# Two token tiles of three half batches by seven block products of half width, in a fused attention and feed-forward kernel

## The chip, the cores and the metric

The kernel runs on one core of one Trainium2 chip. A core has five engines, each with its own instruction queue: TensorE (PE in the profile, with its weight loads as PEld), VectorE (DVE), ScalarE (ACT), GpSimd (POOL) and SyncE (SP), whose queue issues most of the DMA transfers. The metric is the time of one execution in microseconds (us), as the median over runs. Matmul results lie in PSUM banks, which the kernel holds as tiles of 128 x 512 fp32.

## The reference

Two stages, one after the other. Attention is masked by clusters: each query and key goes to the nearest of 16 centroids of its head, and a query sees only keys of its own cluster. The feed-forward stage applies two weight matrices with SiLU between them.

```python
batch, n_heads, seq, head_dim = (4, 8, 768, 64)
...
q_assign = np.argmax(np.einsum('bhsd,hcd->bhsc', q_n, c_n), axis=-1)
k_assign = np.argmax(np.einsum('bhsd,hcd->bhsc', k_n, c_n), axis=-1)
mask = q_assign[:, :, :, None] == k_assign[:, :, None, :]
scores = np.where(mask, scale * np.matmul(q, k.transpose(0, 1, 3, 2)), -1e9)
attn = softmax(scores) @ v
x = np.ascontiguousarray(attn.transpose(0, 2, 1, 3)).reshape(B * S, H * D)   # 3072 x 512
h = x @ w_in                                                                 # 512 x 2048
out = (h * (1.0 / (1.0 + np.exp(-h)))) @ w_out                               # 2048 x 512
```

## The kernel before

**Tiling.** The work is cut into eight half batches (b, c): batch b of 4, half c of its 768 tokens, 384 tokens each. For each half batch and head pair there are score units (`qk_mm`, two matmuls `pS` of 384 columns), an exponential each on ScalarE (`exp`, tile `P`), the product with the values (`pv`, tile `pO`, 36 matmuls of 65 columns), a normalisation on VectorE (`norm`) and a transpose into `xts` (`xn_d` by DMA, or `xn_t` and `xn_ev`). There are 192 score units, 24 per half batch, numbered in order.

The feed-forward stage of a half batch has two kinds of pieces. A hidden unit `unit_a` is one of 16 blocks of 128 hidden features: four matmuls `ph` of 384 columns, tanh on ScalarE, and a gate on VectorE that writes the block into `gt` (f16, 16 blocks x 384 tokens). A part `part_b` is a quarter of an output tile of 128 tokens x 512 columns: four matmuls `po` with a block of `gt` as weights and 512 columns of `wout_s` streaming. Four parts make one tile, VectorE copies it from PSUM with a factor 0.5 into `ot`, and SP stores it. A half batch has three such tiles (`NM` = 3).

**Cluster codes.** For each query and key job a load (`load`, tile `raw`), a split into two f16 halves (`hi`, `lo`, tile `hl`), a transpose by DMA (`xpose`, tile `ab`), logits (`psN`), sums, maxima and comparisons on VectorE, and a way back into `ab` (`cd_mm` and `cd_ev`, or for later jobs `c_scale` on GpSimd, `c_xpose` on SP, `c_move` on GpSimd) give the mask, which is added by the same matmul that makes the scores.

**Order.** Up to the first 26 or so score units the order is a list written out by hand (`plan`). From there a planner in Python emits the instructions: it keeps a clock per engine, lists of pieces with a ready time, a length and a due time (`add`, `run`), and for TensorE chooses at each step among scores, transposes, hidden units and parts (`options`). Loads and the jobs' chains are dated by the number of a score unit (`date`). The spacing of score units is steered by `PACE`. What the planner emits is fixed in the program; on the chip each engine works off its own queue in that order and waits on semaphores.

**Buffers.** Four PSUM banks (`free`) go round among `ph`, `po`, `pO`, `psN`, `psC` and `px`; two double banks hold the scores. `raw` has eight buffers, `hl` four, `ot` three, `gt` two.

**End.** After the last scores the remaining parts are put between the hidden units of half batch (3,1) (`unit_aa` makes two blocks at once), then its three output tiles follow, the last one in three column pieces (L986).

## Time and profile before

| what | us |
|---|---|
| median of 3 runs | 305.29 |
| lowest and highest run | 304.9, 306.08 |
| span of the profiled execution | 302.8 |
| TensorE busy in it | 294.3 |
| ScalarE busy | 211.2 |
| VectorE busy | 200.6 |
| GpSimd busy | 69.1 |

The span runs from the first to the last instruction of the program in one profiled execution; the run times hold in addition what lies before and after it. A row of the timeline gives a start, a length, engine, source line, operation, tiles and count. The length of a matmul is that of one pass through the array, and matmuls overlap: how fast they follow each other is read from their starts. A row of the list of groups gives the count, then busy time and the mean length of one in ns, then the engine's idle time before such instructions and what ended it.

### The profile page before, as it was taken

The numbers are of one execution on the slowest core, as the hardware profiler recorded it, in microseconds if no ns is written. First come the engines' busy times: TensorE is split into PE (matmuls) and PEld (weight loads), VectorE is DVE, ScalarE is ACT, GpSimd is POOL, SyncE is SP. The second block draws the span as 40 slices with busy tenths as digits, with TensorE's granted clock in tenths as the row PEclk, the third lists the DMA queues.
The fourth block names the chain that finished last, engine by engine and source line by source line (L and its number), as shares of the span: only waits on it lengthen the run. The fifth ranks groups of instructions, "written<-read, shape, count | busy, mean of one in ns | idle before, by whom it ended". The sixth has DMA issues, their size and how long they took to land.

```text
span 302.8 us, 7783 instructions
## 1 busy us (share of the span) xinstructions
PE 294.3 (97%) x3113; PEld 186.3 (62%) x3113; DVE 200.6 (66%) x427; ACT 211.2 (70%) x341; POOL 69.1 (23%) x131
## 2 busy tenths in 40 slices
PE   7899989999999999999999999999999999999995
PEld 3777756566675566655666556655666556755644
DVE  5987669699995679855889468873464136522732
ACT  5899889653985688955698468955897568951520
POOL 2984700101310141433333324122100000000000
PEclk9999999999999999999999999999999999999999
DMA  7888999999794879869999998953101120010102
GB/s 212 249 185 183 201 254 209 247 252 223 174 184 117 218 188 151 197 160 176 231 187 226 187 179 211 163 82 97 38 0 55 46 82 13 16 50 35 37 35 69
DMA packets 74387, 44.07 MB, mean 146 GB/s; under 512 B 54352, under 2 KB 69360, under 8 KB 74352
## 3 DMA queue, kind: packets, MB, share of 16 engines
q1 hardware_dynamic: 69264, 35.16, 50.8%
q0 software_dynamic: 4800, 8.13, 14.2%
q8 instruction: 24, 0.39, 0.6%
q10 hardware_dynamic: 288, 0.30, 0.3%
q14 instruction: 11, 0.09, 0.1%
HBM read 27.30 MB, written 6.29 MB: 111 GB/s over the span
## 4 chain that ended last, share of the span: by engine, by line
PE 87%; ACT 4%; DVE 4%; DMA 2%; SPq 1%; issue 1%; DVEq 0%; ACTq 0%
PE ph L410 25%; PE po L468 25%; PE pS L343 19%; PE pO L360 11%; PE psN L175 3%; ACT P L348 3%; PE phs L448 2%; DVE hl L127 1%; PE po L986 1%; DMA raw<-in_k_dram 1%; DMA xt<-xn 1%; SPq L107 1%; ACT ab L159 1%; PE px L382 0%; SPq L228 0%
## 5 line engine op out<-in xcount | busy, mean ns | idle before, releaser
L348 ACT ACTIVATE P<-pS 128x768 f16<-128x768 f32 x192 | 155.6, 821 | 55.1 <-PE pS L343 54.7
L343 PE MATMUL pS<-ab 128*128 128x384 f16 x384 | 93.2, 326 | 0.5 <-ACT P L348 0.4
L410 PE MATMUL ph<-xt,win_s 128*128 128x384 f16 x480 | 92.4, 326 | 1.2 <-DVE gt L433 0.8
L468 PE MATMUL po<-wout_s,gt 128*128 128x512 f16 x368 | 90.8, 379 | 0.0
L433 DVE SCALAR_TENSOR_TENSOR gt<-tn,ph 128x384 f16<-128x384 f32 x120 | 64.0, 549 | 23.7 <-ACT tn L430 23.1
L430 ACT ACTIVATE tn<-ph 128x384 f32<-128x384 f32 x120 | 60.1, 507 | 10.1 <-PE ph L410 8.1
L410 PEld LDWEIGHTS <-win_s 128*128 128x128 f16 x480 | 46.2, 98 | 31.4 <-issue 2.0
L468 PEld LDWEIGHTS <-gt 128*128 128x128 f16 x368 | 35.0, 98 | 33.8
L343 PEld LDWEIGHTS <-ab 128*128 128x128 f16 x384 | 34.7, 98 | 26.1 <-issue 1.1
L360 PEld LDWEIGHTS <-P 128*128 128x128 f16 x1152 | 39.8, 97 | 4.4
L360 PE MATMUL pO<-vt,P 128*128 128x65 f16 x1152 | 41.2, 193 | 0.0
L127 DVE SCALAR_TENSOR_TENSOR hl<-raw,hl 128x768 f16<-128x768 f32 (+3 forms) x35 | 31.9, 916 | 0.8 <-ACT hl L118 0.4
L475 DVE TENSOR_SCALAR ot<-po 128x512 f32<-128x512 f32 x23 | 15.8, 688 | 23.3 <-PE po L468 23.1
L290 POOL CAST vt<-vn 128x384 f16<-128x384 f32 x32 | 17.9, 558 | 46.4 <-DMA vn<-in_v_dram 41.9
L187 DVE TENSOR_REDUCE L<-psN 128x192 f32<-128x384 f32 (+1 forms) x27 | 14.9, 550 | 15.1 <-PE psN L175 15.0
L232 POOL DMA_DIRECT2D ab<-cdt x16 | 8.9, 557 | 58.0 <-PE pS L343 28.0
L175 PEld LDWEIGHTS <-ab 128*128 128x128 f16 x458 | 17.2, 97 | 5.0 <-DMA ab<-hl 1.1
L175 PE MATMUL psN<-stk,ab 128*128 128x32 f16 (+1 forms) x458 | 18.6, 188 | 0.5 <-DMA ab<-hl 0.5
L370 DVE RECIPROCAL zr<-pO 128x6 f32<-128x6 f32 x32 | 6.2, 193 | 19.2 <-PE pO L360 18.8
L372 DVE TENSOR_TENSOR xn<-pO,zr 128x384 f16<-128x384 f32 x32 | 17.8, 557 | 1.1
L219 POOL TENSOR_SCALAR od<-od 128x96 f16<-128x96 f16 x16 | 9.2, 576 | 36.0 <-DVE od L212 35.9
L122 DVE TENSOR_SCALAR hl<-raw 128x768 f16<-128x768 f32 x24 | 13.9, 580 | 0.6 <-DMA raw<-in_k_dram 0.6
(75 smaller groups left out, 155.8 us busy)
## 6 DMA issues: line engine op xcount, KB each, us to landing
raw<-in_k_dram SPq DMA_DIRECT2D x31, 192.0 KB, 3.8
out_dram<-ot SPq DMA_DIRECT2D x23, 256.0 KB, 2.3
raw<-in_q_dram SPq DMA_DIRECT2D x24, 192.0 KB, 3.6
vn<-in_v_dram SPq DMA_DIRECT2D x16, 192.0 KB, 4.5
vn<-in_v_dram POOLq DMA_DIRECT2D x16, 192.0 KB, 3.7
win_s<-in_moe_w_in_dram POOLq DMA_DIRECT2D x8, 256.0 KB, 6.7
wout_s<-in_moe_w_out_dram POOLq DMA_DIRECT2D x4, 512.0 KB, 18.2
raw<-in_q_dram SPq DMA_DIRECT2D x2, 384.0 KB, 4.3
```

Of the source, the lines that this page charges most:

```text
L127: nc.vector.scalar_tensor_tensor(out=hl[:, s, 1, :], in0=raws[job.name][:, s, :], scalar=QS, in1=hl[:, s, 0, :], op0=ALU.mult, op1=ALU.sub ...
L175: nc.tensor.matmul(L[:, n % g, :, n // g], ab[:, i, :], stk[:, job.groups[i // 3][0], x : x + w], start=(x == 0), stop=(x + w == 2 * HC),)
L290: nc.gpsimd.tensor_copy(vt[:, :, 0:D], vns.pop(i))
L343: nc.tensor.matmul(pS[:, e, 0:HALF], abs_[kj.name][:, kn, :], rhs, start=True, stop=True)
L348: nc.scalar.activation(out=P, in_=pst.pop(u)[:, :, 0:HALF], func=AF.Exp, bias=0.0, scale=ESC)
L360: nc.tensor.matmul(o[:, (2 * t + h) * VW : (2 * t + h + 1) * VW], Ps[i + h, c, j // 2][:, j % 2, ts(t, 128)], vtb[(i + h) % 13][:, j, 0:VW ...
L372: nc.vector.tensor_tensor(out=xn, in0=ov[:, :, 0:D], in1=zr.unsqueeze(2).to_broadcast([128, 2 * NM, D]), op=ALU.mult)
L410: nc.tensor.matmul(ph[:, 0:HALF], win_s[:, r, ts(fb, 128)], xts[b, c][:, r, :], start=(r == 0), stop=(r == NR - 1))
L430: nc.scalar.activation(out=tn, in_=ph[:, 0:HALF], func=AF.Tanh, bias=0.0, scale=0.5)
L433: nc.vector.scalar_tensor_tensor(out=gt[:, fb, :], in0=tn, scalar=1.0, in1=ph[:, 0:HALF], op0=ALU.add, op1=ALU.mult)
L468: nc.tensor.matmul(po, gts[b, c][:, fc, ts(t, 128)], wout_s[:, fc, :], start=(fc == 0), stop=(fc == NFB - 1))
L475: nc.vector.tensor_scalar(out=ot, in0=po, scalar1=0.5, scalar2=None, op0=ALU.mult)
```

## The change

In the half batches (2,0), (2,1) and (3,0), two of the three token tiles (256 tokens) are no longer made by 2 x 4 parts, but by seven products of Strassen's scheme in Winograd's form. `gt` of the two tiles is seen as a 2 x 2 block matrix (token tile by half of the hidden features), `wout_s` as 2 x 2 (half of the hidden features by half of the 512 output columns). A product is eight matmuls of 256 columns over half of the hidden features (`Pair.product`). Six products add up in one PSUM bank X, in the order 1, 6, 5, 7, 4, 3, and product 2 goes to a second bank Y; between them ScalarE and VectorE read the banks (`p1`, `c11`, `u2`, `c22`, `c12`), as the partial sums are the outputs. The third tile of these half batches is still made by four parts, which the planner may put between the products.

What the products need beside is made on VectorE: four sums of `gt` blocks per pair (`Pair.sums`, 128 x 1024 f16 each, two of them in place), and once the four sums of `wout_s` blocks (`tw_piece`, ten instructions over 32 blocks of 128 x 256), from score unit 122 on. The weights' sums lie in the buffers `raw0` to `raw4` and in `zz`, a copy of X in `hl3`; the loads from the 19th on therefore turn in `raw5` to `raw7`, their halves in `hl0` to `hl2`, and the two code tiles share four buffers.

The factor 0.5 of the output moves into the values' column of ones, which becomes 2, so that the attention output is halved; tanh takes scale 1.0, and the output is copied unscaled. In the planner some pieces of VectorE may go to ScalarE (`either`), some constants have other values (`PACE` 1.34 in place of 1.40), and products have their own rules. The three last output tiles are made as before.

```diff
+    EARLY = H + 2 + H
+
+    def raw_tag(n):
+        return f"raw{n % 8 if n < EARLY else 5 + n % 3}"
 
     def load(job, eng=nc.sync):
-        raw = mp.tile([128, 12, D], f32, name="raw", tag="raw", bufs=8)
+        n = len(raws)
+        raw = mp.tile([128, 12, D], f32, name="raw", tag=raw_tag(n), bufs=1)
         for dst, ap in job.srcs:
...
+            n = len(hls)
+            hls[job.name] = mp.tile([128, 12, 2, D], f16, name="hl", tag=f"hl{n % 4 if n < EARLY else n % 3}", bufs=1)
...
-        def act():
+        def act(eng="D"):
             ot = mp.tile([128, DM], f32, name="ot", bufs=3)
-            nc.vector.tensor_scalar(out=ot, in0=po, scalar1=0.5, scalar2=None, op0=ALU.mult)
+            if eng == "A":
+                nc.scalar.activation(out=ot, in_=po, func=AF.Copy, bias=0.0, scale=1.0)
+            else:
+                nc.vector.tensor_copy(ot, po)
             done(po)
             nc.sync.dma_start(out[b * S : (b + 1) * S, :].rearrange("(p j) d -> p j d", j=NJ)[:, j, :], ot)
...
+    HK, HD = NFB // 2, DM // 2
+    uus, tws = [], []
+    TW = ((0, 0, 6), (0, 6, 2), (1, 0, 4), (1, 4, 4), (2, 0, 2), (2, 2, 4), (2, 6, 2), (3, 0, 2), (3, 2, 4), (3, 6, 2))
+
+    def tw(n, f, m=1):
+        x = n * HK + f
+        if x < 30:
+            assert x // 6 == (x + m - 1) // 6
+            return tws[x // 6][:, x % 6 : x % 6 + m, :]
+        return zz[:, (x - 30) * HD : (x - 30 + m) * HD].rearrange("p (m e) -> p m e", m=m)
+
+    def tw_piece(n, f, m):
+        if n * HK + f < 30 and len(tws) <= (n * HK + f) // 6:
+            tws.append(mp.tile([128, 6, HD], f16, name="tw", tag=f"raw{len(tws)}", bufs=1))
+        ks, us = slice(f, f + m), slice(HK + f, HK + f + m)
+        lo_, up = slice(0, HD), slice(HD, DM)
+        a = wout_s[:, ks if n == 0 else us, lo_ if n == 3 else up]
+        b_ = tw(0, f, m) if n == 2 else tw(2, f, m) if n == 3 else wout_s[:, ks, up if n else lo_]
+        nc.vector.tensor_tensor(out=tw(n, f, m), in0=a, in1=b_, op=ALU.subtract)
+
+    def uu_tile():
+        uus.append(mp.tile([128, DM + HD], f32, name="uu", tag="hl3", bufs=1))
+        nc.gpsimd.memset(uus[0][:, 0:HD], 0.0)
+
+    class Pair:
+
+        def __init__(self, b, c):
+            self.b, self.c, self.gt = b, c, gts[b, c]
+
+        def sums(self, k):
+            gt = self.gt
+            if k == 1:
+                self.sg = mp.tile([128, 2, HK, 128], f16, name="sg", tag="sg", bufs=1)
+            low, high = slice(0, HK), slice(HK, NFB)
+            a11, a12 = gt[:, low, 128:256], gt[:, high, 128:256]
+            a21, a22 = gt[:, low, 0:128], gt[:, high, 0:128]
+            s1, s2 = self.sg[:, 0], self.sg[:, 1]
+            o, x, y, op = (
+                (s1, a21, a22, ALU.add), (s2, s1, a11, ALU.subtract), (a21, a11, a21, ALU.subtract), (a12, a12, s2, ALU.subtract)
+            )[k - 1]
+            nc.vector.tensor_tensor(out=o, in0=x, in1=y, op=op)
+
+        def product(self, k):
+            gt, lo_, up = self.gt, slice(0, HD), slice(HD, DM)
+            if k == 1:
+                self.X = bank("po")
+            if k == 2:
+                self.Y = bank("po2")
+            o = self.Y[:, lo_] if k == 2 else self.X[:, up if k in (5, 3) else lo_]
+            for f in range(HK):
+                if k in (5, 6):
+                    w, x = self.sg[:, k - 5, f, :], tw(0 if k == 5 else 2, f)[:, 0, :]
+                else:
+                    fc = f if k in (1, 7) else HK + f
+                    w = gt[:, fc, 0:128] if k in (4, 7) else gt[:, fc, 128:256]
+                    x = tw(3 if k == 4 else 1, f)[:, 0, :] if k in (4, 7) else wout_s[:, fc, up if k == 3 else lo_]
+                nc.tensor.matmul(o, w, x, start=(f == 0 and k in (1, 2)), stop=(f == HK - 1), skip_group_check=True)
+
+        def p1(self):
+            self.ot = mp.tile([128, DM], f32, name="ot", bufs=3)
+            nc.scalar.activation(out=self.ot[:, HD:DM], in_=self.X[:, 0:HD], func=AF.Copy, bias=0.0, scale=1.0)
+
+        def c11(self):
+            nc.vector.tensor_tensor(out=self.ot[:, HD:DM], in0=self.Y[:, 0:HD], in1=self.ot[:, HD:DM], op=ALU.add)
+            done(self.Y)
+
+        def u2(self):
+            nc.scalar.activation(out=uus[0][:, HD : HD + DM], in_=self.X, func=AF.Copy, bias=0.0, scale=1.0)
+
+        def rows(self):
+            o = out[self.b * S : (self.b + 1) * S, :].rearrange("(p j) d -> p (j d)", j=NJ)
+            return o, self.c * NM * DM
+
+        def c22(self):
+            nc.vector.tensor_tensor(out=self.ot[:, 0:HD], in0=self.X[:, 0:HD], in1=uus[0][:, DM : DM + HD], op=ALU.add)
+            o, x = self.rows()
+            nc.sync.dma_start(o[:, x + HD : x + HD + DM], self.ot)
+
+        def c12(self):
+            ot = mp.tile([128, DM], f32, name="ot", bufs=3)
+            nc.vector.tensor_tensor(out=ot, in0=self.X, in1=uus[0][:, 0:DM], op=ALU.add)
+            done(self.X)
+            o, x = self.rows()
+            nc.sync.dma_start(
+                o[:, x : x + 3 * DM].rearrange("p (a e) -> p a e", a=2)[:, :, 0:HD], ot.rearrange("p (a e) -> p a e", a=2)
+            )
...
-        nc.vector.memset(vt[:, :, D : D + 1], 1.0)
+        nc.vector.memset(vt[:, :, D : D + 1], 2.0)
...
-    PACE, LEAST, GAIN = 1.40, 12, .03
+    PACE, LEAST, GAIN, WORK = 1.34, 12, .03, 20.05
     HOLD = 6
+    MARGIN = 0.3
+    EARLY_T = 122
...
+    def backlog(eng, t):
+        return max(clock[eng] - t, 0.0) + sum(p[2] for p in lanes[eng] if p[0] <= t + 1.0)
+
+    def either(ready, dve, act, f, then=None, late=0.0):
+        eng = "ACT" if backlog("ACT", ready) + act + MARGIN < backlog("DVE", ready) + dve else "DVE"
+        add(eng, ready, act if eng == "ACT" else dve, lambda: f(eng[0]), then, late)
...
+    tw_at = {}
+    date(EARLY_T - 1, lambda t: add("POOL", t, 0.3, uu_tile))
+
+    def tw_step(n, t):
+        if n < len(TW):
+            add("DVE", t, 0.06 + 0.16 * TW[n][2], lambda: tw_piece(*TW[n]), lambda t: (tw_at.__setitem__(TW[n][:2], t), tw_step(n + 1, t)), 9.0)
+
+    def tw_ready(k):
+        n = {6: 2, 5: 0, 7: 1, 4: 3}.get(k)
+        need = [tw_at.get(x[:2]) for x in TW if x[0] == n]
+        return None if None in need else max(need, default=0.0)
+
+    date(EARLY_T, lambda t: tw_step(0, t))
...
-    turn, po_on = 0, None
+    turn, pairs, at, next_pair, later = 0, {}, {}, [], []
+    paired = {(b, c) for b in range(2, B) for c in range(2)} - {(B - 1, 1)}
...
+    def sums_from(b, c, t):
+        pr = pairs[b, c]
+
+        def step(k, t):
+            add("DVE", t, 0.65, lambda: pr.sums(k), lambda t: (tell(b, c, f"s{k}", t), step(k + 1, t) if k < 3 else None), k - 1.0)
+
+        step(1, t)
 
...
+            if fb == NFB - 1 and (b, c) in paired:
+                if all("over" in at[x] for x in pairs if x != (b, c)):
+                    sums_from(b, c, t)
+                else:
+                    next_pair.append((b, c))
...
+                if (b, c) in paired:
+                    pairs[b, c], at[b, c] = Pair(b, c), {}
+                    qb.extend([(b, c, "p", k) for k in (1, 2, 6, 5, 7, 4, 3)] + [(b, c, NM - 1, n) for n in range(4)])
+                else:
+                    qb.extend((b, c, t_, n) for t_ in range(NM) for n in range(4))
...
+    def follow(it):
+        b, c, _, k = it
+        pr = pairs[b, c]
+
+        def told(name):
+            return lambda t: tell(b, c, name, t)
+
+        def then(t):
+            tell(b, c, f"p{k}", t)
+            if k == 1:
+                add("ACT", t + 0.2, 0.40, pr.p1, told("c1"))
+            elif k == 2:
+                when(b, c, ("p2", "c1"), lambda t: add("DVE", t + 0.2, 0.45, pr.c11))
+                when(b, c, ("p2", "s2"), lambda t: add("DVE", t + 0.06, 0.65, lambda: pr.sums(4), told("s4"), 1.0))
+            elif k == 5:
+                add("ACT", t + 0.2, 0.61, pr.u2, told("u2"))
+            elif k == 7:
+                add("DVE", t + 0.2, 0.45, pr.c22, lambda t: (tell(b, c, "c22", t), sent(t)))
+            elif k == 3:
+                tell(b, c, "over", t)
+                if next_pair:
+                    sums_from(*next_pair.pop(), t)
+                add("DVE", t + 0.2, 0.69, pr.c12, sent)
+
+        return then
...
+    def part_ready(it, bank_at):
+        b, c, t_, n = it
+        if t_ != "p":
+            need = [gate_at.get((b, c, fb)) for fb in range(4 * n, 4 * n + 4)] + ([bank_at] if n == 0 else [])
+        elif n in (1, 2):
+            need = [gate_at.get((b, c, fb)) for fb in range(HK * (n - 1), HK * n)] + [bank_at]
+        else:
+            names = {6: ("c1", "s2"), 5: ("s1",), 7: ("u2", "s3"), 4: ("c22",), 3: ("c22", "s4")}[n]
+            need = [at[b, c].get(x) for x in names] + [tw_ready(n)]
+        return None if None in need else max(need)
...
-        if unit < NU and unit - 2 in exp_at and 6 * pv_next > unit - 15:
+        if unit < NU and unit - 2 in exp_at and 6 * pv_next > unit - 11:
...
-        if qb and (po_on or bank_at is not None):
-            b, c, t_, n = qb[0]
-            need = [gate_at.get((b, c, fb)) for fb in range(4 * n, 4 * n + 4)]
+        if qb:
             a_soon = qa and x_at[qa[0][:2]] <= t + 0.5
-            if None not in need and (len(qb) > HOLD or not a_soon):
-                found.append((3 if turn < 4 else 2, max(need + ([] if po_on else [bank_at])), 0.863, "b"))
+            opened = qb[0][3] != (1 if qb[0][2] == "p" else 0)
+            ahead = next((k for k, q in enumerate(qb) if (q[2] == "p") != (qb[0][2] == "p")), None)
+            for k in (0, ahead):
+                if k is not None and (k or opened or len(qb) > HOLD or not a_soon):
+                    r = part_ready(qb[k], bank_at)
+                    if r is not None:
+                        found.append((3.5 if k else 3 if turn < 4 else 2, r, 0.874 if qb[k][2] == "p" else 0.863, ("b", k)))
```

68 lines of the change are left out of this document (44 added, 24 removed).

## The prediction

> **What bounds the kernel now.** The first part of the profile page comes first, then the TensorE clock row, then the chain of work that ended last.
>
> ```profile
> span 302.8 us, 7783 instructions
> ...
> PE 294.3 (97%) x3113; PEld 186.3 (62%) x3113; DVE 200.6 (66%) x427; ACT 211.2 (70%) x341; POOL 69.1 (23%) x131
> ...
> PEclk9999999999999999999999999999999999999999
> ...
> PE 87%; ACT 4%; DVE 4%; DMA 2%; SPq 1%; issue 1%; DVEq 0%; ACTq 0%
> ```
>
> TensorE (PE) is busy for 97% of the span at full clock and makes 87% of the chain. An average can hide a stage with another limit, so the table of busy time by stretch is next. Its columns are the stretch, its length, the busy time of each engine, the clock, the DMA share and GB/s.
>
> ```profile
> 0.00:57.00 57.00, 52.67 (x707) 36.73 (x708) 44.47 (x117) 47.59 (x81) 25.24 (x42) 1.00 0.96 210
> 57.00:190.00 133.00, 132.09 (x1414) 83.29 (x1413) 103.39 (x208) 95.09 (x150) 37.82 (x75) 1.00 0.91 196
> 190.00:289.00 99.00, 99.00 (x917) 60.28 (x916) 48.80 (x97) 68.01 (x111) 6.05 (x14) 1.00 0.22 53
> ```
>
> TensorE idles in the first 57 us, whose order is written out by hand and stays. From 57 to 190 us it is idle 0.9 us, while the DMA engines are 91% busy. From 190 to 289 us it never idles, VectorE (DVE) is half free and DMA nearly empty. The three pairs that change lie in that last stretch. So the time is the sum of the matmuls' spacings, and the question is what matmuls the change removes and what waits it puts between them.
>
> "Busy" overlaps pipelined matmuls, so spacings are read from starts, in the timeline of TensorE (start, length, instruction, count):
>
> ```profile
> 240.32 1.26 PE L360 MATMUL pO<-vt,P 128*128 128x65 f16 x36
> 241.41 0.49 PE L343 MATMUL pS<-ab 128*128 128x384 f16 x2
> ...
> 244.98 1.03 PE L468 MATMUL po<-wout_s,gt 128*128 128x512 f16 x4
> 245.84 0.49 PE L343 MATMUL pS<-ab 128*128 128x384 f16 x2
> ...
> 279.82 1.46 PE L410 MATMUL ph<-xt,win_s 128*128 128x384 f16 x8
> 281.12 1.46 PE L448 MATMUL phs<-xt,win_s 128*128 128x384 f16 x8
> ...
> 288.92 7.07 PE L468 MATMUL po<-wout_s,gt 128*128 128x512 f16 x32
> 295.82 3.70 PE L986 MATMUL po<-wout_s,gt 128*128 128x320 f16 x48
> ```
>
> A 512-column matmul takes (295.82 - 288.92)/32 = 0.2156 us, its weight load included; a 384-column one (281.12 - 279.82)/8 = 0.1625; a 65-column one (241.41 - 240.32)/36 = 0.0303.
>
> **The change, part by part.** *Products.* Per pair, 32 matmuls of 512 columns (two tiles, 16 blocks) become 56 of 256 columns (7 products of 8). No row has 256 columns. From 512 and 384 the slope is 0.0531/128 = 0.000415 us a column, so 0.1625 - 128 x 0.000415 = 0.109; from 65 and 384 it is the same, 0.109. Bounds: half of the 512-column spacing, 0.1078, below; the 65-column spacing plus 191 columns at 0.2156/512, 0.111, above. I take 0.1094: a product is 0.875 us, a pair 56 x 0.1094 = 6.13 in place of 32 x 0.2156 = 6.90. Saved 0.77 a pair, **2.3 us for three** (2.1 to 2.6 by the bounds).
>
> The Trainium skill, "TensorE: Matmul & The Clock Gate", section Back-to-back issue gap, speaks against this: it gives streams of load and matmul about 81 ns at 128 columns and 131 ns at 512, so a matmul of half the width costs much more than half. Interpolated (an estimate), 256 columns would be 98 ns, a pair 5.5 in place of 4.2 us, and the change a loss of 3.9. The trace disagrees: 215.6 ns at 512, 30.3 at 65.
>
> *VectorE sums* are new: four per pair over 128x1024 f16, and 32 blocks of 128x256 f16 of the weights. No row has two f16 inputs in SBUF. The nearest (the first is the view of one line, with duration min/median/max):
>
> ```profile
> L127 DVE SCALAR_TENSOR_TENSOR hl<-raw,hl x35: 350/951/1298, 4.0 to 198.0; 128x768 f16<-128x768 f32 x26, 128x576 f16<-128x576 f32 x7, 128x384 f16<-128x384 f32 x1, 128x192 f16<-128x192 f32 x1
> ```
> ```profile
> L161 DVE COPY ab<-pTk 128x768 f16<-128x768 f16 x7 | 3.8, 549 | 0.5 <-PE pTk L150 0.5
> L433 DVE SCALAR_TENSOR_TENSOR gt<-tn,ph 128x384 f16<-128x384 f32 x120 | 64.0, 549 | 23.7 <-ACT tn L430 23.1
> L430 ACT ACTIVATE tn<-ph 128x384 f32<-128x384 f32 x120 | 60.1, 507 | 10.1 <-PE ph L410 8.1
> L348 ACT ACTIVATE P<-pS 128x768 f16<-128x768 f32 x192 | 155.6, 821 | 55.1 <-PE pS L343 54.7
> L475 DVE TENSOR_SCALAR ot<-po 128x512 f32<-128x512 f32 x23 | 15.8, 688 | 23.3 <-PE po L468 23.1
> ```
>
> Scaled by columns, a sum takes 0.549 x 1024/768 = 0.73 us at the rate of the f16 copy, or 0.951 x 1024/768 = 1.27 at that of the two-input line with an f32 input. I take 0.73, since types and layout are the copy's. The Trainium skill, "VectorE: DVE Perf Modes", section Side-by-side, lets two-input 16-bit work pass two elements a cycle; 1024 columns would be some 0.7 us (an estimate). All sums together: 12 x 0.73 + 8192 x 0.549/768 = 8.8 + 5.9 = 14.7 us. VectorE is free for 50 of the 99 us after 190, and some 30 us of matmuls stand between the scores of unit 122 and the first product that reads a sum of weights, so I cost them at nothing. Without that cover (each gate behind a sum holds a PSUM bank) a sum delays TensorE by up to its own 0.73.
>
> *Evictions.* Six of 0.688 us become three sets of two reads of PSUM by ScalarE and three by VectorE. In the changed order ScalarE (ACT) also takes four further output evictions, one code tile and one transposed block. ACT is free for 31 of the last 99 us; no cost, but each can stand ahead of an exponential (0.821) that TensorE awaits.
>
> *Waits inside a pair.* Product 6 needs the second sum. In pairs (2,1) and (3,0) the order puts a product, a score pair, a part, a product and a score pair between the last hidden unit and it: 0.875 + 0.325 + 0.862 + 0.875 + 0.325 = 3.26 us. The chain is 0.16 (matmul length 0.326 less spacing) + 0.51 tanh + 0.55 gate + 2 x 0.73 = 2.68: 0.58 to spare, or 0.24 late behind an exponential. Pair (2,0) has over 6 us there. Product 7 needs ScalarE's copy of the bank, about 0.61 us (0.507 plus 128 columns at (0.821 - 0.507)/384); in (2,1) a part and two score pairs, 1.51 us, stand before it, the chain with an exponential ahead is 0.16 + 0.82 + 0.61 = 1.59. So margins are near zero: 0 to 0.8 a pair; I take **+0.2** in all.
>
> *Smaller buffers.* The last 16 loads turn in 3 buffers in place of 8, their halves in 3 in place of 4. In SP's changed order none of those loads waits for an engine, so the transposes and stores queued behind them aren't held: no cost. A load that did wait would hold SP's whole queue.
>
> *The order from 57 us on* is made anew, with its DMA issues. TensorE lost time there only at four places: at 71, 73 and 145 us at or before a hidden unit, whose bank or input was late, and at 143 us at logits whose transposed input had not landed:
>
> ```profile
> 71.38 2.41 PE L410 MATMUL ph<-xt,win_s 128*128 128x384 f16 x12
> 73.62 0.28 PE L241 MATMUL psC<-ident,om 128*96 128x128 f16 x2
> 74.02 1.30 PE L410 MATMUL ph<-xt,win_s 128*128 128x384 f16 x7
> ...
> 142.53 0.49 PE L343 MATMUL pS<-ab 128*128 128x384 f16 x2
> 143.53 0.52 PE L175 MATMUL psN<-stk,ab 128*128 128x32 f16 x12 [0.51 <-DMA ab<-hl]
> ...
> 145.08 1.77 PE L410 MATMUL ph<-xt,win_s 128*128 128x384 f16 x8
> 146.68 0.49 PE L343 MATMUL pS<-ab 128*128 128x384 f16 x2
> ```
>
> Starts less spacings: 2.24 - 1.95 = 0.29; 0.40 less two short ones (0.11) = 0.29; 1.00 - 0.325 = 0.68; 1.60 - 1.30 = 0.30; together 1.56. For the 0.68, SP's queue shows what stood ahead of the late transpose:
>
> ```profile
> 135.47 1.17 SPq L228 DMA_TRANSPOSE cdt<-od  x1
> 136.73 0.53 SPq L477 DMA_DIRECT2D out_dram<-ot  x1
> 137.35 1.86 SPq L136 DMA_TRANSPOSE ab<-hl  x1
> ```
>
> In the changed order it stands ahead of both, up to 1.88 us sooner. Against that, matmuls counted at their spacings put the scores of unit 102 3.0 us earlier than before (133.2 in place of 136.2), so data are wanted earlier too. All gone would be -1.56, twice as much +1.56; I take **-0.3**.
>
> *Sum*, against the profiled execution's own span: 302.8 - 2.3 + 0.2 - 0.3 = 300.4. The median of the runs, 305.29, lies 2.5 above that span, for start and end that the change doesn't touch: **302.9 us**.
>
> **The rivals.**
>
> *Half-rate sums* (slower). At 1.27 us a sum, the chain to product 6 with an exponential ahead is 0.16 + 0.82 + 0.51 + 0.55 + 2.54 = 4.58, 1.32 over the 3.26, in two pairs: +2.6, so 305.29 - 2.3 + 2.6 = 305.6. It decides from 1.19 us a sum on, where two waits eat the 2.3. For it: the only two-input rows run at 1.25 ns a column (0.951/768); against it: they all read f32 or PSUM.
>
> *Data come no sooner than before* (slower). If the stretch from 57 to 190 us is held by DMA, TensorE waits out the 3.0 us by which the scores of unit 102 moved up: 305.29 - 2.3 + 3.0 = 306.0; it decides from 2.3. For it: a share of 0.91 and one wait on a transpose; against it: that was 0.68 us in 133, and loads are dated by unit, so they move up too.
>
> *The gain is waited away in the pairs* (no change): 0.6 late at product 7 or 6 in each, 1.8 in all, 304.8. For it: margins of 0.58 and -0.08; against it: exponentials are ahead only part of the time, ACT being 69% busy there (68.01 of 99).
>
> *A narrow matmul costs its weight load besides* (slower). With a load's own length added to each narrow matmul,
>
> ```profile
> L468 PEld LDWEIGHTS <-gt 128*128 128x128 f16 x368 | 35.0, 98 | 33.8
> ```
>
> a pair is 56 x 0.207 = 11.6, +4.7 each, 319.4; it decides from 6.90/56 = 0.123 us a matmul. The 65-column row, load included, excludes it. The flat spacing that the Trainium skill gives (page and section above) would fall on this side too.
>
> **How the numbers follow.** Forecast, with sums and waits as costed: 0.75. Waited away 0.11; data no sooner 0.08; half-rate 0.05; flat matmuls 0.01. About 0.5%, 1.53 us, is what a measurement here can tell from no change: under 303.76 is faster, over 306.82 slower. The forecast's own spread runs from 302.9 - 0.3 - 0.2 - 1.26 = 301.1 (2.6 saved, no waits, the whole 1.56 back) to 302.9 + 0.2 + 0.2 + 1.0 = 304.3 (2.1 saved, waits doubled, 0.7 more lost from 57 us on); nearly all of it lies under 303.76, 0.72, and half of the waited-away case, where only some of its waits fall, adds 0.06: faster 0.78. Half-rate and data cases lie about 306 and spill over 306.82 with less than half; with the flat matmuls slower is 0.07. Same is the rest, 0.15. The range, 301.4 to 304.9, holds the forecast and the waited-away case.
>
> **What would show it.** Right: 168 matmuls of 256 columns, eight of them starting 0.87 us before the next group; 272 matmuls of 512 columns left on the output line in place of 368; sums near 0.73 us; no idle row of TensorE on VectorE or ScalarE between 190 us and the end; a span near 300.4. Wrong: sums over 1.19 us; gaps before products 6, 7 or 4; starts of logits or scores after a DMA between 57 and 190 us that add to more than 2 us; a matmul spacing over 0.12.

## The result and the profile after

| | before | after |
|---|---|---|
| median of the runs, us | 305.4 (4 runs) | 312.29 (4 runs) |
| lowest and highest, us | 304.9, 306.08 | 307.86, 314.94 |
| profiled execution, us | | 307.86 |
| span of the profiled execution, us | 302.8 | 306.1 |

The changed kernel is slower in these runs: the ratio of its time to that of the kernel before is 1.0129, with a 95% interval of 1.0082 to 1.0175, where 0.992 was predicted. Three of its four runs had a mean granted clock of 0.987 to 0.994 in place of 0.999, and the two slowest of them stay out of that ratio, as does each run over 1.5% above the fastest of its kernel in every ratio below, so the median stands higher than the ratio says.

The page of the changed kernel, the lines that were shown of the kernel before:

```profile
span 306.1 us, 7968 instructions
...
PE 293.0 (96%) x3185; PEld 193.4 (63%) x3185; DVE 213.1 (70%) x446; ACT 217.5 (71%) x353; POOL 70.7 (23%) x132
...
PE 71%; DMA 13%; DVE 5%; ACT 5%; issue 3%; POOL 1%; SPq 1%; DVEq 0%; POOLq 0%; ACTq 0%
```

TensorE is busy 1.3 us less (293.0 for 294.3), and the span is 3.24 us longer (306.08 for 302.84 before rounding). The chain that ended last now runs through transfers for 13% of the span, where it was 2%, and through TensorE for 71%, where it was 87%. The busy time by stretch says where:

```profile
0.00:57.00 57.00, 51.40 (x696) 36.23 (x697) 43.74 (x115) 46.72 (x79) 25.87 (x42) 1.00 0.95 203
57.00:190.00 133.00, 129.54 (x1385) 80.90 (x1383) 104.72 (x205) 95.61 (x150) 36.72 (x73) 1.00 0.93 193
190.00:289.00 99.00, 99.00 (x1013) 68.69 (x1012) 58.89 (x117) 73.02 (x121) 8.11 (x17) 1.00 0.26 61
```

In the last stretch, where the products stand, TensorE never idles, as before. From 57 to 190 us it idles 3.46 us in place of 0.91, and in the first 57 us 5.60 in place of 4.33.

"Busy" hides part of it, so I also added up, over all matmuls, the time from one start to the next beyond the spacing that its width needs (0.2158 us at 512 columns, 0.1625 at 384, 0.1092 at 256, 0.056 at 128, 0.0303 at 65). This is called lost time below.

| lost by TensorE, us | 0 to 57 | 57 to 100 | 100 to 150 | 150 to 190 | from 190 | last start to end of span |
|---|---|---|---|---|---|---|
| before | 7.74 | 0.64 | 0.99 | 0.00 | 0.05 | 3.51 |
| after | 9.43 | 1.54 | 0.01 | 3.23 | 0.11 | 4.23 |

The sum of the spacings themselves fell by 2.38 us (the last start 301.85 - 14.32 lost, against 299.33 - 9.42; the first start, at 1.18 us, is the same in both). So the 3.24 us come out: -2.38 of matmuls, +1.69 in the first 57 us, +3.15 from 57 to 190, +0.06 behind it, +0.72 at the end.

The 4.78 us that the changed kernel loses from 57 to 190 us are for the most part of three kinds. TensorE loses 0.80 and 0.36 at 84 and 86 us ahead of matmuls that wait on a gate (the last section says what held VectorE there). It loses 1.14 and 0.36 at 154 and 157 us, again on gates, on a chain that starts at a late load. And it loses 0.67 and 1.03 where it waits on a transfer itself, once for a cluster code and once for a transposed attention output:

```profile
168.12 0.50 PE L349 MATMUL pS<-ab 128*128 128x384 f16 x2 [0.51 <-DMA ab<-cdt]
182.81 0.32 PE L416 MATMUL ph<-xt,win_s 128*128 128x384 f16 x1 [0.86 <-DMA xt<-xn]
```

The largest of these waits shows how a transfer reaches TensorE by way of VectorE. The chain of waits passes here (start, length, what):

```profile
148.36 4.24 DMA raw<-in_k_dram
152.72 0.56 DVE hl L128
153.28 0.46 DVE gt L439
```

and the timelines of VectorE and of TensorE show the same place:

```profile
150.55 0.56 DVE L439 SCALAR_TENSOR_TENSOR gt<-tn,ph 128x384 f16<-128x384 f32 x1 [0.92 <-ACT tn L436]
152.72 0.56 DVE L128 TENSOR_SCALAR hl<-raw 128x768 f16<-128x768 f32 x1 [1.62 <-DMA raw<-in_k_dram]
153.20 0.55 DVE L439 SCALAR_TENSOR_TENSOR gt<-tn,ph 128x384 f16<-128x384 f32 x1
```
```profile
152.01 0.81 PE L416 MATMUL ph<-xt,win_s 128*128 128x384 f16 x4
153.80 0.48 PE L416 MATMUL ph<-xt,win_s 128*128 128x384 f16 x2 [0.97 <-DVE gt L439]
```

The split of a load (`hl<-raw`, L128) is at the head of VectorE's queue at 151.11 (150.55 + 0.56), 2.8 us after its load was issued at 148.36; the load takes 4.24 us, so VectorE stands still for 1.62. The gate behind it has its input since 152.38 (tanh began at 151.89 and takes 0.49), but it waits its turn; it frees the PSUM bank of the next hidden unit, and TensorE loses 1.14 us. The gate starts at 153.20, so VectorE's wait accounts for at most 0.82 of that (153.20 - 152.38). TensorE's row names the gate, and only VectorE's own row names the transfer. A like wait of 1.61 us ahead of the split at 146.57 cost TensorE nothing. In the kernel before, the load of 148.36 was issued at 147.64, and its split came to the head of VectorE's queue 5.1 us after that, with no wait:

```profile
152.45 0.36 DVE L212 TENSOR_TENSOR od<-L,mxn 128x192 f16<-128x192 f32 x1
152.73 0.55 DVE L122 TENSOR_SCALAR hl<-raw 128x768 f16<-128x768 f32 x1
```

Over the stretch from 57 to 205 us, the groups of VectorE's splits (count, busy time, mean ns, idle time of the engine just before them and what ended it), first before, then after:

```profile
L122 DVE TENSOR_SCALAR hl<-raw 128x768 f16<-128x768 f32 x20 | 11.7, 585 | 0.6 <-DMA raw<-in_k_dram 0.6
```
```profile
L128 DVE TENSOR_SCALAR hl<-raw 128x768 f16<-128x768 f32 x20 | 12.8, 642 | 4.3 <-DMA raw<-in_k_dram 4.3
```

And the transfers took longer (KB each, median us from issue to landing), before and after:

```profile
raw<-in_k_dram SPq DMA_DIRECT2D x19, 192.0 KB, 3.4
```
```profile
raw<-in_k_dram SPq DMA_DIRECT2D x19, 192.0 KB, 4.2
```

### The profile page after: what moved, and what is told of

Read it like the earlier page. It is cut to its first block, busy times and chain, and to the rows that moved or that the text cites. A ratio compares the mean times of both kernels' runs of the same rounds, so it can differ in the third digit from the quotient of the medians.

```text
span 306.1 us, 7968 instructions
## 1 busy us (share of the span) xinstructions
PE 293.0 (96%) x3185; PEld 193.4 (63%) x3185; DVE 213.1 (70%) x446; ACT 217.5 (71%) x353; POOL 70.7 (23%) x132
## 4 chain that ended last, share of the span: by engine, by line
PE 71%; DMA 13%; DVE 5%; ACT 5%; issue 3%; POOL 1%; SPq 1%; DVEq 0%; POOLq 0%; ACTq 0%
PE ph L416 21%; PE pS L349 15%; PE po L474 15%; PE pO L366 10%; PE po L546 6%; DMA ab<-cd 3%; DMA raw<-in_k_dram 3%; ACT P L354 3%; PE psN L181 2%; DMA xt<-xn 2%; PE phs L454 2%; DVE hl L133 2%; DMA raw<-in_q_dram 1%; DVE gt L439 1%; DMA out_dram<-ot 1%
## 5 line engine op out<-in xcount | busy, mean ns | idle before, releaser
L474 PE MATMUL po<-wout_s,gt 128*128 128x512 f16 x272 | 68.0, 379 | 0.0
L474 PEld LDWEIGHTS <-gt 128*128 128x128 f16 x272 | 25.8, 98 | 25.4 <-issue 1.1
L133 DVE SCALAR_TENSOR_TENSOR hl<-raw,hl 128x768 f16<-128x768 f32 (+3 forms) x35 | 32.7, 936 | 1.3 <-ACT hl L124 0.8
L296 POOL CAST vt<-vn 128x384 f16<-128x384 f32 x32 | 18.7, 584 | 48.5 <-DMA vn<-in_v_dram 48.4
L128 DVE TENSOR_SCALAR hl<-raw 128x768 f16<-128x768 f32 x24 | 15.0, 627 | 4.3 <-DMA raw<-in_k_dram 4.3
L484 DVE COPY ot<-po 128x512 f32<-128x512 f32 x13 | 9.0, 691 | 11.5 <-PE po L474 11.2
```

The source lines that it names most:

```text
L133: nc.vector.scalar_tensor_tensor(out=hl[:, s, 1, :], in0=raws[job.name][:, s, :], scalar=QS, in1=hl[:, s, 0, :], op0=ALU.mult, op1=ALU.sub ...
L296: nc.gpsimd.tensor_copy(vt[:, :, 0:D], vns.pop(i))
L474: nc.tensor.matmul(po, gts[b, c][:, fc, ts(t, 128)], wout_s[:, fc, :], start=(fc == 0), stop=(fc == NFB - 1))
```

## The experiments

The theory after the result: the planner's new constants (`PACE`, the look-ahead and the weights of the stock, which no run here takes apart) put the scores up to 3 us earlier into a stretch whose DMA engines are full, while the planner still believes its own landing times; late loads then stand in VectorE's queue in front of gates. The rivals: the smaller and moved buffers, the pieces moved to ScalarE, and, for the first 57 us and the end, the longer program.

**The changed kernel once more** (`again`), beside the next three on one chip.

> The changed kernel itself once more, beside the kernel before. Theory 1 (the planner's new constants ask for scores up to 3.0 us sooner in the stretch from 57 to 190 us, where the DMA engines are full, and TensorE waits for late transfers) and theory 2 (three raw and hl buffers hold loads) both expect what was seen, 307.9 to 315 us, with waits of TensorE on DMA between 80 and 190 us. A rival says that run was a disturbance: then 302 to 304.

Measured: 307.04 us (302.96 to 310.41, 11 runs), ratio 1.0027 (0.9993 to 1.0062), clocks 0.987 to 1.0. The median is 1.9 us over the 305.12 of the kernel before beside it, but the interval of the ratio holds 1, so these runs by themselves don't show a loss beyond doubt. The times of the changed kernel spread over 7 us, where the kernel before stays within 303.86 to 307.12 in 33 runs beside it.

The profiled execution of this run took 305.39 us, and little of the loss of the first profile is in it. VectorE's splits wait 0.7 us on loads in place of 4.3, the loads take 3.6 us in place of 4.2, and TensorE loses 1.9 us from 57 to 190, where the kernel before loses 1.63:

```profile
L128 DVE TENSOR_SCALAR hl<-raw 128x768 f16<-128x768 f32 x21 | 12.9, 616 | 0.7 <-DMA raw<-in_k_dram 0.7
```

Its span, 303.6 us, is longer than that of the kernel before by what it loses in the first 57 us (9.9 for 7.74) and at the end (4.12 for 3.51). So one program has the waits on loads in one execution and hardly in another, and a single profile can't say how much of the median they make.

**Old constants alone** (`old_const`):

```diff
-    PACE, LEAST, GAIN, WORK = 1.34, 12, .03, 20.05
+    PACE, LEAST, GAIN, WORK = 1.40, 12, .03, 20.8
-        ... 6 * pv_next > unit - 11:
+        ... 6 * pv_next > unit - 15:
-                stock = 1.253 * len(qa) + 0.868 * len(qb) + WORK * (unit // 24 - released)
+                stock = 1.302 * len(qa) + 0.863 * len(qb) + WORK * (unit // 24 - released)
```

> The changed kernel with the planner's constants of before (spacing of scores 1.40, look-ahead 15, the old weights of the stock); products, buffers and the choice between VectorE and ScalarE stay. Theory 1: most of the loss goes, 303 to 304 us, no wait on DMA of a microsecond before 190 us. Theory 2 (buffers): still 307 or more.

Measured: 304.61 us (302.95 to 307.08), ratio 0.9977 (0.9947 to 1.0006). The median is 2.4 us under that of `again`, though over the 303 to 304 that the theory expected, and the intervals of the two ratios overlap. In its profile no wait of VectorE on a load is left from 57 to 205 us. TensorE still loses 3.0 us from 57 to 190, about half of it, 1.54, at 86 us on a transposed input, so waits on transfers are not the new constants' alone.

**New constants alone, in the kernel before** (`before_new_const`): the same edit the other way round, with no product in the kernel.

> The kernel before with the new constants alone (spacing 1.34, look-ahead 11, new weights of the stock). Theory 1: slower than before by 3 to 6 us, 308 to 311, with the waits on DMA between 80 and 190 us. Theory 2: within 1 us of before.

Measured: 307.3 us (304.99 to 308.95), 2.2 over the 305.12 of the kernel before beside it; ratio 1.0041 (1.0008 to 1.0073). So the constants cost time without any product, though less than the 3 to 6 us that the theory expected. The trace has the same wait, VectorE's splits first, and then the two engines at the largest place:

```profile
L122 DVE TENSOR_SCALAR hl<-raw 128x768 f16<-128x768 f32 x20 | 12.8, 639 | 4.1 <-DMA raw<-in_k_dram 4.1
```
```profile
193.57 1.02 DVE L433 SCALAR_TENSOR_TENSOR gt<-tn,ph 128x384 f16<-128x384 f32 x2 [1.14 <-ACT tn L430]
196.13 0.56 DVE L122 TENSOR_SCALAR hl<-raw 128x768 f16<-128x768 f32 x1 [1.54 <-DMA raw<-in_k_dram]
196.72 0.96 DVE L127 SCALAR_TENSOR_TENSOR hl<-raw,hl 128x768 f16<-128x768 f32 x1
197.60 1.48 DVE L433 SCALAR_TENSOR_TENSOR gt<-tn,ph 128x384 f16<-128x384 f32 x3
```
```profile
195.61 0.81 PE L343 MATMUL pS<-ab 128*128 128x384 f16 x4
198.20 1.25 PE L360 MATMUL pO<-vt,P 128*128 128x65 f16 x36 [1.78 <-DVE gt L433]
```

After VectorE's 1.54 us on the load, the second half of the split (0.96) also goes ahead of three gates; TensorE, out of free banks, loses 1.95. At 153 us it loses 1.61 in the same way, behind a split that waited 1.66 for its load. In this profile the two make most of the 5.29 us lost after 57 us.

**The order of before up to unit 122, then the new one** (`hybrid`): products, small buffers and the weights' sums stay; constants and the choice of ScalarE are the new ones from unit 122 on only.

```diff
+    SWITCH = 122
-        eng = "ACT" if backlog("ACT", ready) + act + MARGIN < backlog("DVE", ready) + dve else "DVE"
+        eng = "ACT" if unit >= SWITCH and backlog("ACT", ready) + act + MARGIN < backlog("DVE", ready) + dve else "DVE"
+                if unit < SWITCH:
+                    stock = 1.302 * len(qa) + 0.863 * len(qb) + 20.8 * (unit // 24 - released)
+                    due = t >= scored + min(max(1.40 + GAIN * (stock - LEAST - 0.867 * (24 - unit % 24)), 0.8), 2.2)
+                else:
...
```

> The changed kernel with the order of before up to score unit 122 (old constants and no move of VectorE work to ScalarE until there), new constants from there on. Theory 1: about 2.3 us under before, 303 us. Theory 2: the reduced buffers hold loads before unit 122 all the same, 306 or more.

Measured: 303.3 us (302.21 to 304.74), ratio 0.9945 (0.992 to 0.9969): faster than both kernels. VectorE's splits wait for nothing, 0.0 in place of 4.3:

```profile
L128 DVE TENSOR_SCALAR hl<-raw 128x768 f16<-128x768 f32 x20 | 11.9, 596 | 0.0
```

**The buffers alone** (`before_bufs`): no products, the order of before, the buffers of the changed kernel.

> No products: the order of before (old constants, no choice of ScalarE), with the changed kernel's buffers (raw 8 then 3, hl 4 then 3, shared code tiles) and so its addresses in SBUF. Theory 1 (new constants alone cost the loss): as before, within 0.7 us, and 5.4 us lost by TensorE in the first 57 us as before. Theory 2b (the profiles of the kernels with these buffers lost 0.8 to 2.4 us more in the first 57 us, where the order of instructions is the same, so the buffers or their addresses cost it): 1 to 2 us slower than before, with scores waiting about 1 us for a code tile near 27 us.

Measured: 304.74 us, ratio 0.9989 (0.9965 to 1.0014). The buffers cost nothing that these runs can tell. **Buffers moved back** (`hybrid_layout`): `hybrid` with the halves of loads, the operands `ab` and the values' loads at the SBUF addresses that they have in the kernel before.

> The hybrid (order of before up to score unit 122, then the products) with the four hl buffers side by side, which puts hl, ab and vn at the addresses that they have in the kernel before. Theory 2b by addresses: the wait near 27 us goes and it is 1 us faster than the hybrid was, 302.3 or so. Theory 1 alone: as the hybrid, 303.3.

Measured: 304.0 us, ratio 0.9954 (0.9927 to 0.9981), not to be told from `hybrid`.

**Nothing moved to ScalarE** (`no_either`):

```diff
-        eng = "ACT" if backlog("ACT", ready) + act + MARGIN < backlog("DVE", ready) + dve else "DVE"
+        eng = "DVE"
```

> The changed kernel without the planner's choice of ScalarE for evictions: new constants and products stay. Theory 1: still slower than the hybrid by some 2 us, 305 to 306, since the constants bring the scores forward all the same. Theory 3 (the moves to ScalarE make the loss): 303.5.

Measured: 306.54 us (302.43 to 311.42), much as the 307.04 of `again`; five of its eleven runs took 308.6 to 311.4. By the medians the moves make little difference. The ratio, 0.9981 (0.9944 to 1.0017), lies about as far under the 1.0027 of `again` as that of `old_const` does, and all these intervals overlap. So the moves to ScalarE aren't excluded as a part of the cause. The profiled execution took 310.22 us and shows what one of the long runs has; the other four weren't traced. VectorE waits for no load in it (0.0 us from 57 to 205), with the new constants in place. The wait is TensorE's own, on a transfer:

```profile
177.10 0.65 PE L416 MATMUL ph<-xt,win_s 128*128 128x384 f16 x3
181.35 0.48 PE L416 MATMUL ph<-xt,win_s 128*128 128x384 f16 x1 [3.60 <-DMA xt<-xn]
181.62 1.91 PE L474 MATMUL po<-wout_s,gt 128*128 128x512 f16 x4
```

and the busy times of the stretches around it (the column 1.00, 0.55, 0.77 is the granted clock):

```profile
175.00:180.00 5.00, 2.75 (x15) 1.31 (x14) 4.33 (x10) 2.01 (x3) 1.13 (x2) 1.00 0.81 164
180.00:185.00 5.00, 3.65 (x26) 2.02 (x26) 1.92 (x3) 1.28 (x2) 2.23 (x5) 0.55 0.87 222
185.00:190.00 5.00, 5.00 (x40) 2.94 (x38) 3.58 (x7) 2.12 (x4) 1.50 (x3) 0.77 0.53 85
```

One transpose of the attention output came late and held a hidden unit back for 3.76 us. Before that wait was over the clock had fallen to half: the four 512-column matmuls from 181.62 to 183.33 take 0.43 us each in place of 0.216. Over the three rows, half clock for (0.45 x 5 + 0.23 x 5)/0.5 = 6.8 us; the wait of 3.76 us costs a further 2.9 us after it. The first profile of the changed kernel has the same wait, ahead of the same hidden unit, at 181.79, where it lasts 1.03 us and leaves the clock alone.

**Old constants, nothing moved to ScalarE, to the end** (`hybrid_999`): `hybrid` with the switch past the last unit.

> The products with the old constants and no choice of ScalarE to the end. Theory 1: as the hybrid or a little over it, 303 to 304, since the products' 2.3 us stay and after 190 us DMA is nearly empty.

Measured: 304.67 us, ratio 0.9994 (0.9964 to 1.0024). That is over the 303 to 304 expected: with the old planning all the way the products' gain doesn't show. The profile loses only 1.57 us after 57 us, but 9.2 in the first 57 us, and its end is 4.97 us long in place of 3.51, which brought up the next question.

**The end.** In `hybrid`, VectorE's last copy waits for a store of one of the three output buffers:

```profile
299.76 0.23 DVE L1199 COPY ot<-po 128x64 f32<-128x64 f32 x1 [1.54 <-DMA out_dram<-ot]
```

Transfers in a window of 5 us at the end, first `hybrid` (from 295 us), then the kernel before (from 296 us):

```profile
q8 instruction: 1, 0.02, 1.1%
...
out_dram<-ot SPq DMA_DIRECT2D x1, 256.0 KB, 4.1
```
```profile
out_dram<-ot SPq DMA_DIRECT2D x1, 256.0 KB, 2.0
```

The queue q8 brings TensorE's instructions in blocks of 16 KB; the longer program needs 25 where that of before needs 24, and the 25th comes while the last full output tile is being stored. That store takes 4.1 us in place of 2.0. It takes 3.3 to 4.3 in all ten profiles of kernels with products, and 2.0 in the four with 24 blocks. So, with buffers of their own for the last two pieces (`hybrid_tail`):

```diff
-        ot = mp.tile([128, DM], f32, name="ot", bufs=3)
+        ot = mp.tile([128, DM + HD], f32, name="otl", tag="hl0" if x == DM else "hl1", bufs=1) if x > 5 * DM // 8 else mp.tile([128, DM], f32, name="ot", bufs=3)
```

> The kernel called hybrid (products, before's order up to unit 122), with one edit: the last two column pieces of the last output tile (128 and 64 columns) get buffers of their own, in place of the two oldest of the three output buffers. In every profile of a kernel with products the 64-column copy at the end waits 0.8 to 1.8 us for an earlier store to land, and in none without them. Theory that this wait sets the end: the copy waits only on the last matmul (0.17 us, as before), the span ends 3.3 to 3.5 us after the last matmul in place of 4.65, and the time is 303.3 - 1.2 = 302.1, ratio to the kernel before about 0.990. Rival, that the slow store itself sets the end, whatever the copy waits for: the copy is early, the chain ends with that store, and the time stays 303.3, ratio 0.9945.

Measured: 302.73 us (301.34 to 304.03), ratio 0.991 (0.9875 to 0.9946). The profiled span is 300.0, the copy waits 0.17 us on its matmul, and the span ends 3.51 us after the last start of a matmul in place of 4.80. The interval just reaches the 0.9945 of `hybrid`, which the rival expected, so the wait is gone, but the gain in time isn't clear of the noise:

```profile
296.75 0.23 DVE L1199 COPY otl<-po 128x64 f32<-128x64 f32 x1 [0.17 <-PE po L1193]
```

**A longer program alone** (`before_pad`): the kernel before with 72 small matmuls added among the last column pieces.

```diff
+        for fc in range(24):
+            nc.tensor.matmul(po[:, 0:16], gts[B - 1, 1][:, fc % 8, 0:128], wout_s[:, fc % 8, 0:16], start=True, stop=True, skip_group_check=True)
```

> The kernel before with 72 more matmuls of 16 columns (and their weight loads) among the last three column pieces, whose results are overwritten: TensorE's program is as long as that of the changed kernel, and nothing else differs. Theory that the longer program costs in the first 57 us (where all seven profiles with products lose 8.3 to 9.9 us of TensorE time and all three without them 7.7 to 8.0): 8.3 to 9.9 lost there. Rival, that it is something else of the products' kernels (the place of tiles in SBUF) or chance: 7.7 to 8.0 lost there. The added matmuls themselves cost 72 times 0.025 to 0.1, 2 to 7 us, all after 295 us. By the first theory the 25th fetch of 16 KB of TensorE's instructions also comes while the last stores are under way, and one of them takes 3 to 4 us in place of 2.

Measured: 307.58 us, ratio 1.0073 (1.0049 to 1.0096). It loses 8.68 us in the first 57, as the longer-program theory asked; but `hybrid_tail`, as long a program, loses 7.71 there, and `new_const_slack` below, with the short program, 8.63. So what is lost in the first 57 us (7.7 to 9.9 in all profiles) isn't set by the length of the program alone. The 25th block comes in this kernel too, though later, beside the store of 64 KB: that takes 2.5 us in place of 1.5, and the stores of 256 KB ahead of it 2.0. So a slow store goes with the fetch, without any product.

**Splits dated later** (`after_load_slack`): the changed kernel, all its constants kept, with one number changed: the planner places the split 1.9 us after it believes that the load has landed.

```diff
-            t = max(t, loaded[job.name] + 0.4)
+            t = max(t, loaded[job.name] + 1.9)
```

> The changed kernel with one edit: the planner dates the split of a load's f32 tile into f16 halves 1.9 us after the time at which it believes the load has landed, in place of 0.4. The scores keep their lead (3.1 us at unit 102, 2.3 at unit 126). Theory that the loss is a late load at the head of VectorE's queue, with the gates of the hidden units behind it: VectorE's idle time before the split falls from 4.3 us (changed kernel) or 4.1 (before with the new constants) to under 1 in the stretch from 57 to 205 us, TensorE loses under 2.5 us there in place of 4.8, and the time is 304 to 305.5. Rival, that the lead itself asks for data sooner than the DMA engines bring them, wherever the wait shows: the waits move to transposes, logits or scores, and the time stays at 306 to 307.5.

Measured: 303.95 us (303.18 to 305.39, 8 runs), ratio 0.996 (0.993 to 0.9989), clocks 0.997 to 1.0. The scores keep their lead, yet VectorE doesn't wait in this profile:

```profile
L128 DVE TENSOR_SCALAR hl<-raw 128x768 f16<-128x768 f32 x20 | 12.7, 634 | 0.0
```

TensorE loses 1.25 us from 57 to 190 in place of 4.78. The rival, that the lead itself asks too much of the DMA engines, expected 306 to 307.5, and the time speaks against it; the interval of the ratio lies under that of `again`, if only just. But the edit makes the order anew from the first split on. TensorE's own waits on transfers at 168 and 183 us are gone too, and whether they hung on the late loads stays open.

**The same edit without products** (`new_const_slack`), to tell the wait from the luck of another order: `before_new_const` with that one line.

> The kernel before with the planner's new constants (no products, 307.3 us without the further edit), and the same edit as in the kernel called after_load_slack: the split of a load is dated 1.9 us after its believed landing, in place of 0.4. The scores keep their lead (3.1 us at unit 102, 3.3 at unit 126). Theory that late loads at the head of VectorE's queue are what the constants cost: VectorE's idle time before the split falls from 4.1 us to under 1, TensorE loses under 2.5 us after 57 us in place of 5.3, and the time is 304.9 to 305.9, that of the kernel before. Rival, that the changed kernel only happened on a better order with that edit: 306.5 to 307.5, with the waits in other places.

Measured: 306.26 us (305.32 to 308.75), ratio 1.0019 (0.9991 to 1.0047), between the two expectations. The wait falls from 4.1 us to 1.6, where under 1 was expected, and the time lost after 57 us from 5.29 to 1.70:

```profile
L122 DVE TENSOR_SCALAR hl<-raw 128x768 f16<-128x768 f32 x20 | 11.5, 573 | 1.6 <-DMA raw<-in_k_dram 1.5
```

So the edit works on that wait in this kernel too, but by the ratios the runs recover about half of the loss, and the two intervals overlap. Whether something else in the new constants costs time stays open.

**Both edits in the changed kernel** (`slack_tail`).

> The changed kernel with two edits: the split of a load dated 1.9 us after its believed landing, as in the kernel called after_load_slack (303.95 us), and buffers of their own for the last two column pieces, as in the kernel called hybrid_tail. Theory that both waits are what keeps the products' gain away: the 64-column copy waits 0.17 us, the span ends 3.3 to 3.5 us after the last matmul in place of 4.8, and the time is 302.6 to 302.9, ratio to the kernel before about 0.991, near the 302.9 of the prediction. Rival, that the end is set by the slow store whatever the copy waits for: 303.9.

Measured: 302.88 us (301.75 to 304.1), ratio 0.9908 (0.9874 to 0.9943), the time that was predicted for the change. In its profile, of a run of 304.09 us, VectorE waits on loads again, in spite of the edit, and TensorE loses 2.1 us from 57 to 190, 0.97 of them on a gate behind a split that waited 1.22:

```profile
L128 DVE TENSOR_SCALAR hl<-raw 128x768 f16<-128x768 f32 x20 | 11.2, 561 | 2.9 <-DMA raw<-in_k_dram 2.9
```

So later splits don't take the wait out of every execution. Of the kernels with the new constants throughout, the wait came to 4.3, 0.7, 4.1 and 0.0 us without the edit and to 0.0, 1.6 and 2.9 with it. What the edit gains is shown by the times of the runs; that it gains it by this wait is argued.

The copy waits 0.17 us, but the span ends 4.07 us after the last start: with the fetch among them the last stores, of 160, 64 and 32 KB, take 2.7, 2.2 and 1.7 us, where they took 1.8, 1.5 and 1.5 in the kernel before; so part of the slow store's cost stays.

## Why the prediction was wrong

The prediction of 302.9 us fails above all at one step: *the order from 57 us on*, costed at -0.3 us with bounds of -1.56 and +1.56. From 57 to 190 us the profile lost 4.78 us in place of 1.63, so the step was +3.15 in the profiled execution, outside its bounds. In the profile of `again` it was only +0.3. That the remade order costs time over many runs is shown by `before_new_const` (ratio 1.0041, without any product) and by `hybrid`, which keeps the old order up to unit 122 and is 3.7 us faster than `again` in the median. Which of its waits makes the median is shown only in part. Three things were wrong in the step. The bounds were taken from the waits that the old order had, and a new order can make new ones. The step noted that the scores of unit 102 come 3.0 us earlier, and gave that no price in the sum. And the argument, made against the rival, that "loads are dated by unit, so they move up too" was not held against the order: the load before the wait at 151 us was issued 0.72 us later than before (148.36 for 147.64), while its split came to the head of VectorE's queue 1.6 us sooner (151.11 for 152.73).

The rival *data come no sooner than before*, with a chance of 0.08, came nearest; its 306.0 us stands beside 307.86 in the profiled run and 307.04 in the median of eleven. That its 3.0 us agree with the 3.15 of the profile is partly luck, since the next profile has 0.3. Its mechanism was a part of it. It had TensorE itself wait on data, and TensorE does so for 1.70 us in the first profile and for 3.76 in that of `no_either`. The largest single wait of the first profile came by way of VectorE, whose row names the load, while TensorE's rows name a gate. The sign set for the rival, starts of logits or scores after a DMA adding to over 2 us, would have missed it: of scores there is 0.67 us, and the rest stands before hidden units.

The other steps:

- *Products*: right. The 168 matmuls of 256 columns follow each other at 0.1092 us (0.1094 was taken), and 272 of 512 columns are left. A product takes 0.87 us:

```profile
269.57 1.04 PE L546 MATMUL po<-wout_s,gt 128*128 128x256 f16 x8
270.44 0.49 PE L349 MATMUL pS<-ab 128*128 128x384 f16 x2
```

All spacings together fell by 2.38 us, 2.3 were forecast; the two rivals in which a narrow matmul costs more than its columns fall.

- *VectorE sums*: right, 0.69 us where 0.73 was taken. The estimate of some 0.7 us, worked out from the Trainium skill (page "VectorE: DVE Perf Modes", section Side-by-side), agrees:

```profile
L530 DVE TENSOR_TENSOR sg<-gt 128x1024 f16<-128x1024 f16 x3 | 2.1, 692 | 0.1
```

- *Waits inside a pair*: 0.2 were taken, and TensorE lost 0.11 us in all after 190 us, against 0.05 before. So the sums and the evictions there are hidden, as costed; half-rate sums and a gain waited away in the pairs both fall.
- *Evictions and smaller buffers*: costed at nothing. `before_bufs` bears the buffers out; for the moves to ScalarE `no_either` leaves it open (ratio 0.9981 for 1.0027, with overlapping intervals).
- *Start and end, that the change doesn't touch*: wrong, and in the profile of `again` the larger part of the miss. The added instructions bring a 25th fetch into the last stores, +0.72 us in the span (+0.61 in `again`). The first 57 us cost 1.69 more in this profile and 2.1 in `again`, but kernels of both kinds and lengths show such values, and what sets them stays open.

What put the median at 312.29, 4.4 over the profiled run, was not traced in these very runs. An estimate from the trace of `no_either`: a mean clock of 0.987 over 300 us means some 7.8 us at half clock, thus 3.9 us lost, beside the wait ahead of it; the run with 0.987 took 314.04, 6.2 over the profiled one.

## What to carry to other kernels

A queue that is worked off in order passes a late transfer on to everything behind it (here 0.82 us of VectorE's wait of 1.62 reached a gate), so before believing a gain in a stretch with full DMA engines, list for each instruction that reads a fresh load how long after the load's issue it comes to the head of its queue, and compare that with the landing time. A scheduler that dates such readers by a believed landing may need slack for it when its pace is raised: here 1.5 us of it brought the changed kernel from 1.0027 to 0.996 of the time before, about as much as the gain of the cheaper matmuls, and a third as much in the kernel without products. Take more than one profile before blaming a wait on a transfer: the same program had 4.3 us of it in one execution and 0.7 in the next. And bound the cost of a remade order by what its own moves can cost, not by the waits of the old one.

## What the runs showed of the hardware

- A wait of TensorE can cost twice. Around a wait of 3.76 us for a transfer, seen once, the granted clock was 0.5 for 6.8 us, and TensorE lost 2.9 us more after the wait; waits of 1.0 to 1.95 us in other profiles left it at 1.00. The Trainium skill, "TensorE: Matmul & The Clock Gate", section "Part 1: The HAM clock gate", puts the window of the gate at about 3.4 us, and these waits lie on either side of it.
- A fetch of 16 KB of instructions can slow a store: 256 KB took 3.3 to 4.3 us with a fetch beside it (ten profiles) and 2.0 without one (five), and in `before_pad`, without products, the 64 KB store beside the fetch took 2.5 in place of 1.5. The Trainium skill, "Runtime: NRT & Kernel Launch", section Instruction fetch mechanics, gives the same block of 16 KB on a DMA queue, and holds the fetch to be mostly hidden; it is, for TensorE, which lost 0.11 us in all after 190 us in the changed kernel, but not for the store beside it.
- A split of VectorE (f32 to f16, both in SBUF) that takes 0.55 us by itself took 1.72 where GpSimd issued a transfer and cleared a tile, in kernels of either order; TensorE lost up to 1.1 us there. VectorE's row of `before_pad`, then GpSimd's:

```profile
81.51 1.72 DVE L122 TENSOR_SCALAR hl<-raw 128x768 f16<-128x768 f32 x1
```
```profile
81.44 0.55 POOL L285 DMA_DIRECT2D vn<-in_v_dram  x1
81.98 0.83 POOL L799 MEMSET od<- 128x256 f16 x3
82.73 0.61 POOL L285 DMA_DIRECT2D vn<-in_v_dram  x1
```

The split ends at 83.23, GpSimd's issue, clears and second issue at 83.34. That fits the Trainium skill, "SBUF — State Buffer", section "Who interferes with whom", by which the two engines hold a shared pair of ports one at a time. No run here took one of the two away to show it.
